# One PSUM copy of each quad moved from VectorE to ScalarE in a window-attention backward kernel

## The chip, the cores and the metric

The kernel runs on one core of a Trainium2 chip. The metric is the time of one execution on the device in microseconds (us); the median of several runs is compared. The engines are named as the profile names them: PE (matrix engine, PEld its weight loads), DVE (VectorE), ACT (ScalarE), POOL (GpSimd) and SP (the sync engine, which here only issues transfers).

## The reference, cut to what matters

```python
def _fwd_reference(x, wqkv, wo):               # x: 1 x 256 x 256 x 384, bf16
    # 1024 windows of 8 x 8 = 64 tokens, C = 384 channels, one head
    qkv = xw @ wqkv
    q, k, v = qkv[..., :C], qkv[..., C:2*C], qkv[..., 2*C:]
    p = softmax(einsum('bqc,bkc->bqk', q, k) * C ** -0.5)
    o = einsum('bqk,bkc->bqc', p, v) @ wo
...
_out, _vjp = jax.vjp(_f, x, wqkv, wo)
return _out, *_vjp(grad_out)                   # o, dx, dwqkv, dwo
```

## The kernel before, in words

**Algebra.** The weights are multiplied together once: A = Wq Wk^T scaled, B = Wv Wo, and their transposes. Then the scores are x A x^T, the output is P (x B), and the gradient of P is grad_out B^T x^T. Both weight gradients come from two sums over all windows, x^T (dS x) and x^T (P^T grad_out), with dS the gradient of the scores; a few small products after the loop turn them into dwqkv and dwo.

**Tiling.** Two windows make a tile of 128 tokens, four tiles (numbered t = 0 to 3) a quad; there are 128 quads. The order of all five engines' instructions is written out by hand: each engine runs its instructions in the order in which the program gives them. One call of `step` works on three quads at once: stage A on quad i+1, stage B on quad i, stage C on quad i-1.

- Stage A: z = B^T grad_out (`project`, kind 0, line 147, copied by ACT at L161), y = A x (`project`, kind 1, L145, copied by ACT at L163), and `to_tokens`, a transposing DMA of both into `tok`.
- Stage B: scores and dP in one tile `sd` (L147), softmax and its gradient on DVE with one exponential on ACT, giving `Pb` (P) and `ps` (P and dS side by side); u = x B and v = x A^T (`uv`, L147, copied by ACT at L229); `turn`, a transposing DMA of `ps` into `PS`.
- Stage C, `attend`, once for the tiles (0, 1) and once for (2, 3), "first pair" and "second pair". For each of the two tiles: dS x in `pu` (to `Uq`), P u in `po` (the output), P^T grad_out in `pw` (to `Wq`), and dx in `pd`. Each of these is four matmuls on 64 x 64 quarters of the array.
- Filler: a sixth of the sum over three finished quads (`pg`, 12 matmuls, or 24 on halves of the array), added into `GF_acc` by DVE (L304), twice per step.

**Order of a step on PE.** `sd`; eight `uv` products; three z products; a `pg` filler; first pair; three y products; a `pg` filler; second pair. So right behind the first pair's last two matmuls (`token_part` of t1, L258) stands the first y product (L145, with `A_sb`).

**Order inside a pair.** PE: `token_part` of t0 (two matmuls into `pd`), `pu` and `po` of t0, `pw` and `pd` of t0, `pu` and `po` of t1, `pw` and `pd` of t1, `token_part` of t1. DVE: the four copies `Uq` t0 (L274), `Wq` t0 (L277), `Uq` t1 (L281), `Wq` t1 (L284). ACT: two copies of `po` (L264 `o`) and two of `pd` (L264 `d`), which end only with the pair. Before the first pair, ACT's last work is the three z copies (L161); after it come the three y copies (L163). DVE's last work before the first pair is the `GF_acc` addition of the filler.

**The ring.** All PSUM tiles come from one ring of eight banks (tag "r"), 33 tiles a step. A tile's first matmul waits until the reader of the bank's former tile is done. The banks are handed out in the order in which the program releases them. In the program before, the first y product takes the bank of the first pair's `pu` t0 (released by the DVE copy L274), the second y product that of the first `po` (ACT), the third that of `pw` t0 (DVE, L277), and the filler behind them that of the second `po` (ACT). In the second pair, `pw` of t1 takes the bank of that filler (released by DVE, L304).

**Transfers.** SP issues, in this order in every step: `dT` and `xT` (transposing DMAs of grad_out and x for the quad after next, L128), `PS` (L233), four loads of x (L118), and `tok` (L167). POOL issues the stores of both outputs after each pair (six each) and four loads of grad_out.

Of the kernel before, what the change touches and what calls it, by code (L numbers as in the profile page):

```python
# [22 lines left out]
def kernel(  # L23
# [21 lines left out]
    nc = tc.nc  # L45
# [61 lines left out]
    def windows(ap, st, first, count=2):  # L107
        row, col = st["at"]
        return ap[0, row + WIN * first:row + WIN * (first + count), col:col + WIN, :]
# [126 lines left out]
    def turned(st, n, t, h):  # L236
        if n in ("PT", "ST"):
            return st["PS"][h, t, int((n == "ST") == (h == LO)), :]
        return st[n][h, t, :]

    def attend(st, pair):
        if pair[0] == 0:
            st["Uq"] = grp.tile([P, QUAD, C], BF16, tag="Uq", name="Uq")
            st["Wq"] = grp.tile([P, QUAD, C], BF16, tag="Wq", name="Wq")

        def bank(name):
            return ring.tile([P, C], F32, tag="r", name=name)

        def both(straight, crossed, t, outer, **flags):
            for h, o, (dst, lhs, rhs), fl in ((LO, LO, straight, {}), (LO, HI, crossed, flags), (HI, LO, crossed, flags),  # L250
                                              (HI, HI, straight, {})):
                at = dst if dst is not crossed[0] else dst[outer if h == LO else 1 - outer]
                nc.tensor.matmul(at[o, :], lhsT=turned(st, lhs, t, h), rhs=st[rhs][h, t, :],  # L253
                                 **{"start": True, "stop": True, **fl})

        def token_part(t, pd, outer, **flags):
            for w, o in ((0, HI), (1, LO)):
                nc.tensor.matmul(pd[outer if w == 0 else 1 - outer][o, :], lhsT=st["ps"][:, t, w, :],  # L258
                                 rhs=st["tok"][:, :, t, w, :], **flags)

        def keep(name, dst, src):
            for outer in (0, 1):
                sb = ob.tile([P, C], BF16, tag=name, name=name)
                nc.scalar.copy(out=sb[:], in_=src[outer][:])  # L264
                stores.append((dst, sb, outer))

        t0, t1 = pair
        stores = []
        pu = [bank("pu")]
        po = [bank("po") for outer in (0, 1)]  # L270
        pd = [bank("pd") for outer in (0, 1)]
        token_part(t0, pd, 1, start=True, stop=False)
        both((pu[0], "ST", "xq"), (po, "PT", "uq"), t0, 1)
        nc.vector.tensor_copy(out=st["Uq"][:, t0, :], in_=pu[0][:])  # L274
        pw = [bank("pw")]
        both((pw[0], "Pb", "dq"), (pd, "ST", "vq"), t0, 1, start=False, stop=True)
        nc.vector.tensor_copy(out=st["Wq"][:, t0, :], in_=pw[0][:])  # L277
        pu.append(bank("pu"))
        both((pu[1], "ST", "xq"), (po, "PT", "uq"), t1, 0)
        keep("o", out_0, po)  # L280
        nc.vector.tensor_copy(out=st["Uq"][:, t1, :], in_=pu[1][:])  # L281
        pw.append(bank("pw"))
        both((pw[1], "Pb", "dq"), (pd, "ST", "vq"), t1, 0, start=True, stop=False)
        nc.vector.tensor_copy(out=st["Wq"][:, t1, :], in_=pw[1][:])  # L284
        token_part(t1, pd, 0, start=False, stop=True)
        keep("d", out_1, pd)
        for dst, sb, outer in stores:
            if outer:
                nc.gpsimd.dma_start(out=windows(dst, st, 2 * t1 + 1, 1), in_=sb[LO, :])
                nc.gpsimd.dma_start(out=windows(dst, st, 2 * t0, 1), in_=sb[HI, :])  # L290
            else:
                nc.gpsimd.dma_start(out=windows(dst, st, 2 * t0 + 1), in_=sb[:])  # L292
# [22 lines left out]
    def step(c, b, a, ahead):  # L315
# [25 lines left out]
        if ahead is not None:  # L341
            load(ahead)
        filler(1)
        C_(attend, (0, 1))
        split[0] = True
        for mo in range(CK):
            A(project, 1, mo)
        A(to_tokens)
        filler(1)
        split[0] = ALL  # L350
        C_(attend, (2, 3))

    G_ON_PE = 0
# [86 lines left out]
```

## Time and profile before

| what | value |
|---|---|
| median of 4 runs | 2007.19 us (2000.94 to 2009.74) |
| the profiled execution | 2007.31 us, of which the span of the trace is 2005.2 us |
| granted TensorE clock | 0.999 |
| PE, PEld busy | 1970.7 us (98%), 1193.8 us (60%) |
| DVE, ACT, POOL busy | 1318.0 us (66%), 1405.4 us (70%), 1122.4 us (56%) |
| DMA packets' time, SP's queue and POOL's queue | 81.3% and 30.9% of 16 engines' span |
| `Uq` copy L274 on DVE | 256 times, mean 553 ns (median 558 in the first pair, 548 in the second) |
| ACT copies of the same shape (128 x 384, f32 to bf16) | `uq` 483 ns, `vq` 488, `o` 482, `d` 505 |

The profile is one execution. Busy shares are averages over the span; a PE that is busy 98% is not at its peak, because the ends of pipelined matmuls are modelled and overlap. What one step costs is read best from the timeline: from one `sd` to the next, 15.2 us pass in most steps. In timeline rows, the columns are start (us), duration (us), engine, line, operation, tiles and shape, count, and in brackets the idle time before and what ended it.

### The profile page before, as it was taken

What the parts mean: (1) busy time and instruction counts of PE and PEld (TensorE: products, weight loads), DVE (VectorE), ACT (ScalarE), POOL (GpSimd) and SP (SyncE); (2) the same over time, 40 slices, a digit from 0 to 9 for tenths busy, and PEclk for the clock granted to TensorE, in tenths of its full rate; (3) what the DMA queues carried; (4) which work ended last, traced back from release to release, by engine and by line L of the source; (5) the groups of instructions that cost most, each with busy time, mean ns of one, the idle gap of its engine ahead of it and who ended that gap; (6) DMA issues with size and microseconds to landing.
All of it is one profiled execution on the core that took longest, in us unless ns stands there. A gap on an engine that the chain in (4) does not pass through costs nothing. (4 is left out here: it accounts for less than half of the span.)

```text
span 2005.2 us, 52374 instructions
## 1 busy us (share of the span) xinstructions
PE 1970.7 (98%) x19418; PEld 1193.8 (60%) x19418; DVE 1318.0 (66%) x2979; ACT 1405.4 (70%) x3213; POOL 1122.4 (56%) x2054
## 2 busy tenths in 40 slices
PE   8899999999999999999999999999999999999998
PEld 4456556665666665656655666666666566666565
DVE  5666666666666666666666666666666666666666
ACT  5777777676767767767777677677767777777773
POOL 3555555555556555555655565555555556555543
PEclk9999999999999999999999999999999999999999
DMA  9999999999999999999999999999999999999993
GB/s 200 221 211 220 196 221 222 220 215 211 211 218 219 216 214 212 226 210 217 220 211 214 218 217 213 220 218 221 217 204 226 207 222 220 219 215 207 222 204 98
DMA packets 1042272, 425.62 MB, mean 212 GB/s; under 512 B 925792, under 2 KB 1016672, under 8 KB 1042016
## 3 DMA queue, kind: packets, MB, share of 16 engines
q1 hardware_dynamic: 943312, 270.60, 81.3%
q0 software_dynamic: 98304, 151.39, 30.9%
q8 instruction: 152, 2.49, 0.5%
q14 instruction: 104, 0.85, 0.1%
q10 hardware_dynamic: 400, 0.29, 0.0%
HBM read 101.84 MB, written 101.84 MB: 102 GB/s over the span
## 5 line engine op out<-in xcount | busy, mean ns | idle before, releaser
L292 POOL DMA_DIRECT2D out_dram<-o x256 | 139.2, 544 | 714.8 <-ACT o L264 703.1
L264 ACT CAST o<-po 128x384 bf16<-128x384 f32 x512 | 220.4, 482 | 375.6 <-PE pu L253 365.1
L304 DVE TENSOR_TENSOR GF_acc<-pg,GF_acc 128x384 f32<-128x384 f32 x258 | 143.9, 558 | 501.7 <-PE pg L145 343.7
L147 PEld LDWEIGHTS <-xT 128*128 128x128 bf16 x3072 | 291.8, 98 | 182.2
L147 PE MATMUL pj<-B_sb,xT 128*128 128x384 bf16 x1536 | 333.4, 326 | 0.0
L147 PE MATMUL pj<-AT_sb,xT 128*128 128x384 bf16 x1536 | 333.3, 326 | 0.0
L119 POOL DMA_DIRECT2D dq<-in_grad_out_dram x512 | 274.2, 547 | 73.1 <-DMA out_dram<-o 40.9
L147 PE MATMUL pj<-dT,BT_sb 128*128 128x512 bf16 x1152 | 269.7, 379 | 12.8 <-DMA dT<-dq 11.2
L145 PE MATMUL pj<-xT,A_sb 128*64 128x512 bf16 x2304 | 274.4, 381 | 0.6 <-DMA xT<-xq 0.6
L229 ACT CAST uq<-pj 128x384 bf16<-128x384 f32 x512 | 247.4, 483 | 30.5 <-PE pj L147 26.9
L229 ACT CAST vq<-pj 128x384 bf16<-128x384 f32 x512 | 250.1, 488 | 2.7 <-ACT uq L229 0.3
L145 PEld LDWEIGHTS <-xq 128*64 128x64 bf16 x3000 | 210.7, 110 | 46.2
L264 ACT CAST d<-pd 128x384 bf16<-128x384 f32 x512 | 225.7, 505 | 0.3 <-ACT o L264 0.2
L147 PEld LDWEIGHTS <-xq 128*128 128x128 bf16 x1572 | 153.7, 98 | 114.8 <-issue 0.3
L163 ACT CAST yz<-pj 128x512 bf16<-128x512 f32 x384 | 206.7, 633 | 2.4 <-PE pj L145 2.3
L161 ACT CAST yz<-pj 128x512 bf16<-128x512 f32 x384 | 207.0, 643 | 1.9 <-ACT vq L229 1.3
L207 ACT COPY ps<-Pb 64x256 bf16<-64x256 bf16 x256 | 103.2, 403 | 149.7 <-DVE Pb L204 148.2
L145 PEld LDWEIGHTS <-A_sb 128*64 128x64 bf16 x2304 | 156.2, 110 | 84.7 <-issue 1.2
L147 PEld LDWEIGHTS <-BT_sb 128*128 128x128 bf16 x1152 | 111.6, 98 | 138.1 <-DMA dT<-dq 17.6
L147 PE MATMUL pg<-Uq,xq 128*128 128x384 bf16 x1032 | 181.6, 326 | 0.0
L258 PE MATMUL pd<-tok,ps 128*64 128x384 bf16 x1024 | 181.4, 344 | 0.0
L253 PE MATMUL pu<-xq,PS 64*64 64x384 bf16 x1024 | 175.0, 335 | 6.2 <-DMA PS<-ps 6.1
(67 smaller groups left out, 3384.9 us busy)
## 6 DMA issues: line engine op xcount, KB each, us to landing
xq<-in_x_dram SPq DMA_DIRECT2D x512, 96.0 KB, 4.1
dq<-in_grad_out_dram POOLq DMA_DIRECT2D x512, 96.0 KB, 3.9
out_dram<-o POOLq DMA_DIRECT2D x256, 96.0 KB, 4.3
out_dram<-o POOLq DMA_DIRECT2D x512, 48.0 KB, 4.3
out_dram<-d POOLq DMA_DIRECT2D x256, 96.0 KB, 4.5
out_dram<-d POOLq DMA_DIRECT2D x512, 48.0 KB, 4.4
dT<-dq SPq DMA_TRANSPOSE x128, 6.5
xT<-xq SPq DMA_TRANSPOSE x128, 6.8
```

Of the source, the lines that this page charges most:

```text
L119: nc.gpsimd.dma_start(out=dq[:, t, :], in_=windows(grad_out, st, 2 * t))
L145: nc.tensor.matmul(out[h], lhsT=lhsT[:, h], rhs=rhs, start=start, stop=stop)
L147: nc.tensor.matmul(out, lhsT=lhsT, rhs=rhs, start=start, stop=stop)
L161: ENG[EV["z"][mo]](out=yz[:, mo, :, 0:4:3, :], in_=pj[:])
L163: ENG[EV["y"][mo]](out=yz[:, mo, :, 1:3, :], in_=pj[:])
L207: nc.scalar.copy(out=ps[h, :, w, :], in_=Pb[h, :, :])
L229: cp(out=dst[:, t, :], in_=pj[:])
L253: nc.tensor.matmul(at[o, :], lhsT=turned(st, lhs, t, h), rhs=st[rhs][h, t, :], **{"start": True, "stop": True, **fl})
L258: nc.tensor.matmul(pd[outer if w == 0 else 1 - outer][o, :], lhsT=st["ps"][:, t, w, :], rhs=st["tok"][:, :, t, w, :], **flags)
L264: nc.scalar.copy(out=sb[:], in_=src[outer][:])
L292: nc.gpsimd.dma_start(out=windows(dst, st, 2 * t0 + 1), in_=sb[:])
L304: nc.vector.tensor_tensor(out=GF_acc[:, f, ma, :], in0=pw[:], in1=GF_acc[:, f, ma, :], op=ALU.add)
```

## The change

The copy of `pu` into `Uq` for the first tile of a pair (L274) goes to ACT where that tile is t0 = 0, that is in the first pair, and stays on DVE in the second pair. 128 of the 256 copies of that line move. In ACT's order the moved copy stands between the third z copy (L161) and the first `o` copy (L264).

```diff
         both((pu[0], "ST", "xq"), (po, "PT", "uq"), t0, 1)
-        nc.vector.tensor_copy(out=st["Uq"][:, t0, :], in_=pu[0][:])
+        (nc.vector.tensor_copy if t0 else nc.scalar.copy)(out=st["Uq"][:, t0, :], in_=pu[0][:])
         pw = [bank("pw")]
```

The order of PE, SP and POOL does not change, nor the number of waits on PE. Because banks are handed out in the order of release, three of them go to other tiles: the first y product still takes the bank of `pu` t0 (now released by ACT), the second takes that of `pw` t0 (DVE, L277), the third that of the first `po` (ACT), the filler that of the second `po` (ACT). In the second pair `pu` t0 takes the bank of the first pair's `pw` t1 (DVE) and one `po` that of a `pd` of the first pair (ACT); before, it was the other way round.

## Prediction, made before the changed kernel ran

> **What bounds the kernel now.** I read the page first, then the chain of waits, the list of PE's waits, the timeline around the change, and last SP's timeline, because the DMA figure looked suspicious.
>
> ```profile
> span 2005.2 us, 52374 instructions
> PE 1970.7 (98%) x19418; PEld 1193.8 (60%) x19418; DVE 1318.0 (66%) x2979; ACT 1405.4 (70%) x3213; POOL 1122.4 (56%) x2054
> ```
>
> ```profile
> PE pj L147 <- DMA dT<-dq: 11.2, 8, 2.6
> ...
> PE pu L253 <- DMA PS<-ps: 6.1, 5, 2.0
> ```
>
> PE is busy 98%, and the chain that ended last is PE work all through the loop. PE's listed waits (the second fence: us in total, times, longest) are few: 17.3 us for transfers in 13 places of the loop. DVE and ACT have a third of their time free, so what their copies cost in busy time says nothing; what counts is when a copy frees a PSUM bank that PE wants. Such waits need not show in a list of idle time, since modelled ends of matmuls overlap the next start. I therefore looked at starts, around the first pair of one step:
>
> ```profile
> 1006.78 0.56 DVE L304 TENSOR_TENSOR GF_acc<-pg,GF_acc 128x384 f32<-128x384 f32 x1 [1.11 <-PE pg L147]
> ...
> 1006.97 0.35 PE L253 MATMUL pu<-xq,PS 64*64 64x384 bf16 x1
> ...
> 1007.37 0.56 DVE L274 CAST Uq<-pu 128x384 bf16<-128x384 f32 x1
> ...
> 1007.67 0.86 ACT L264 CAST o<-po 128x384 bf16<-128x384 f32 x2 [0.72 <-PE pu L253]
> 1007.73 0.35 PE L258 MATMUL pd<-tok,ps 128*64 128x384 bf16 x2
> ...
> 1007.98 1.27 PE L145 MATMUL pj<-xT,A_sb 128*64 128x512 bf16 x10
> ```
>
> The copy L274 ends at 1007.37 + 0.56 = 1007.93, and 0.05 us later the first y product starts, the tile that takes over this bank. In the trace's records, to the nanosecond, this holds in all 123 undisturbed steps: the product starts 53 to 55 ns after the copy's end, whatever else varies. So it waits for the copy. What would it do if it didn't? Three steps show it, because in them the copy was done early (198 to 1632 ns ahead of the product); this is one:
>
> ```profile
> 69.06 0.56 DVE L274 CAST Uq<-pu 128x384 bf16<-128x384 f32 x1 [0.78 <-PE pu L253]
> ...
> 69.96 0.35 PE L258 MATMUL pd<-tok,ps 128*64 128x384 bf16 x2
> ...
> 70.15 1.68 PE L145 MATMUL pj<-xT,A_sb 128*64 128x512 bf16 x14
> ```
>
> From the second of the two L258 matmuls to the product it is 183, 184 and 184 ns in these three, against 242 to 245 ns (median 243) in the 123 others. The hidden wait is 243 - 183 = 60 ns a step. The steps run at 15,206 ns with a scatter of 1 to 2 ns except where a transfer is late, so such a wait is paid each time.
>
> I computed the same distance, from a bank's release to its next matmul, for all 33 tiles of a step. One other tile is held: `pw` of t1 in the second pair, 54 ns behind the `GF_acc` addition. The next smallest distances are 130 ns (`pw` of t1 in the first pair, behind `GF_acc`) and 161 ns (`sd`, behind the second pair's L274), and then 353 ns.
>
> **What is removed, and what stays.** DVE loses 128 copies of 558 ns, of which its order needs 465 (start to start of the copies behind it). DVE had them between the `GF_acc` addition and `Wq` of t0. It is 66% busy, so this alone is worth nothing. `Wq` of t0 could start 0.3 us earlier; its bank's next user had 881 ns to spare, and as second y product it will still have about 490.
>
> **What is added, and when it is done.** The matmuls of `pu` t0 end, as modelled, 52 ns before DVE starts (1007.32). DVE starts later than it could, because the `GF_acc` addition ends only at 1007.34; on other occasions DVE starts 37 ns behind PE. ACT's shortest distance behind PE is 36 ns. ACT has been idle by then for 413 ns (median, from the end of the third z copy to the start of L274), so it starts about 15 ns earlier than DVE. It then takes 478 to 485 ns for this shape (the `o` and first `uq` copies, whose mean in the page is 482 and 483) against 558. So the bank is free 15 + 75 = 90 ns earlier. From an ACT copy's end to a waiting matmul it is 52 ns (seen at the start of the trace), as from DVE. The product would thus be held for 60 - 90 = -30 ns: no longer at all, and the limit is PE's own 183 ns. Gain: 60 ns, with 30 ns of margin. Bounds: were the ACT copy as slow as the `d` copies (505) or the fourth `uq` (498), the margin shrinks to 10 ns and the gain stays; at 0.55 us it would be 40 ns less. So 20 to 60 ns, and I take 60, the row of the plain copy.
>
> The Trainium skill ("Perfetto Trace Analysis", Optimizing Scalar/DVE Operations) gives an access overhead of about 125 ns for DVE on PSUM and 51 for ACT, twice that in profiled latency. By that, as an estimate, the ACT copy would be 2 x 74 = 148 ns shorter; the rows say 75. The sum would be the same 60 ns, since PE's own 183 ns ends it. The same section would offload to ACT when DVE is saturated; here ACT is the busier one (70% against 66%), so by that advice there is nothing to gain, and what speaks for the change is only the bubble.
>
> **What is pushed back.** On ACT the two `o` copies, two `d` copies and three y copies queue behind the moved one. ACT's copies follow each other at 370 to 375 ns, so the first `o` starts at about 9.65 us after `sd` instead of 9.59: 60 ns later. Who waits for them: the third y product has the first `o`'s bank (it had 471 ns as second product and now comes 650 ns later, so about 1000 ns), the filler the second `o`'s (about 1250). The y copies start about 60 ns later until the third, which waits for PE (its product ends within 20 ns of its start now) and so moves with PE. Its readers, `sd` and the DMA `tok`, see nothing. POOL's stores of the first pair start 60 ns later; POOL idles 4.54 us before them. Cost: 0. In the second pair the swapped banks had 2.8 us to spare.
>
> **Sum.** 123 steps x 60 ns = 7.4 us at PE. The profiled execution took 2007.31 us, 0.1 above the median of 2007.19, so either can be the base: 2007.3 - 7.4 = 1999.9 if all of it arrives.
>
> **What may take it back: the transfers.** SP's timeline is solid:
>
> ```profile
> 999.37 1.19 SPq L233 DMA_TRANSPOSE PS<-ps  x1
> 1000.61 2.50 SPq L118 DMA_DIRECT2D xq<-in_x_dram  x4
> 1003.22 5.40 SPq L167 DMA_TRANSPOSE tok<-yz  x1
> 1008.85 1.92 SPq L128 DMA_TRANSPOSE dT<-dq  x1
> 1010.95 3.73 SPq L128 DMA_TRANSPOSE xT<-xq  x1
> 1014.84 1.19 SPq L233 DMA_TRANSPOSE PS<-ps  x1
> ```
>
> One round follows the other with gaps of 0.04 to 0.23 us, and SP waits for nobody; `PS` is issued 7 to 8 us before PE needs it, with 4.7 us to land. About every thirteenth round takes 18.5 us instead of 15, and most of PE's waits for `dT` or `PS` follow one of these. So SP and PE are nearly balanced. Is SP the true limit? The Trainium skill ("Perfetto Trace Analysis", What "DMA-bound" means) counts a solid issuing track as one of the ways to be bound by DMA; by that the gain would be 0. The trace speaks against it: issue durations stretch and shrink. The five kinds' shortest issues (4.04, 1.41, 1.42, 1.19, 4 x 0.58 us) and gaps sum to 11.2 us. When `PS` is 6.5 to 7.0 us ahead, a round takes 14.7 us in the mean; at 7.5 to 8.0 us, 15.25; above 8, 15.6. SP thus catches up when it falls behind, and 15.15 us a round is inside what it does. Its lead would settle some 0.2 us lower (0.06 us over a slope of 0.33 us a round for each us of lead). Each of 13 waits may grow by up to that, 2.6 us, but most waits have their own jitter; I take 0.5. Bounds: 0, and all 7.4.
>
> Forecast: 2007.3 - 7.4 + 0.5 = 2000.4 us.
>
> **Rivals.**
> - *The transfers keep the time.* SP's mean round, long ones included, is 15.32 us, as is PE's with its waits. If that is a capacity, PE's 60 ns turn into longer waits: 2004 to 2008 us, PE's listed DMA waits rising from 17 towards 25 us. For it: SP never idles. Against: the fast rounds after each long one.
> - *The wait isn't one, or ACT only replaces it.* Either 243 ns is PE's own change between tilings, or ACT frees the bank no earlier. Time 2007. Against the first: three steps at 183; against the second: 75 ns in duration. It would need an ACT copy of over 0.56 us.
> - *Slower: ACT arrives late at the copy.* The place is ACT's queue ahead of L274, the three z copies. They end 0.41 us before `pu` is ready. If they or a wait for the third z copy's `yz` push L274 by more than 0.09 + 0.41 = 0.50 us, the y product waits longer than now, and each further 0.1 us costs 12.3 us: 2013 us at 0.05 beyond. It decides against me only if the z copies move, and nothing in the diff moves them.
>
> **How the numbers follow.** About 0.3% (6 us, 2001.2) is what a measurement of this kernel can tell from no change; single runs before lie 4.4 us around their middle. Bank wait gone and mostly kept: 0.75, giving 1997 to 2003, with 0.63 below 2001.2 and 0.12 above. Transfers keep it: 0.13 (0.11 same, 0.02 slower). No real wait: 0.06, same. ACT late: 0.06, slower. Together faster 0.63, same 0.29, slower 0.08. The likeliest case's own range is 1997 to 2003; to hold 8 in 10 with the transfers' case and run scatter I take 1996.5 to 2007.
>
> **What would show it.** After: L274 on ACT 478 to 505 ns, starting 0.3 to 0.5 us behind the third z copy; 183 to 190 ns from L258 to the first y product; `pw` of t1 in the second pair still 54 ns behind `GF_acc`; steps of 15.146 us; first `o` about 0.06 us later within the step; PE's DMA waits 17 to 21 us. Wrong, if the y product still starts 50 to 55 ns behind the copy, now ACT's, or if the steps are 15.15 us but late transfers eat over 4 us.

## The result, and the profile after

The changed kernel takes 1998.73 us (median of 44 runs) against 2005.66 us for the kernel before, now over 70 runs. The ratio is 0.9968, with a 95% interval of 0.9957 to 0.9979: 6.4 us less. The forecast was 6.9 us less, from a base of 2007.3 us to 2000.4; of the 1.7 us between 2000.4 and 1998.73, 1.5 are the base, which came out at 2005.66 over more runs. The profiled execution has a span of 1998.1 us against 2005.2. The row of busy times of the page after:

```profile
PE 1963.3 (98%) x19418; PEld 1122.8 (56%) x19418; DVE 1258.4 (63%) x2851; ACT 1453.9 (73%) x3341; POOL 1122.4 (56%) x2054
```

DVE lost 60 us of busy time, ACT took on 49, and PE is busy 98% as before. None of these shares tells of a gain. PEld's fall by 71 us is a trace of it, as the third experiment shows. The timeline after, around the first pair of one step, answers to the one of before:

```profile
1015.28 0.35 PE L253 MATMUL pu<-xq,PS 64*64 64x384 bf16 x1
...
1015.68 0.48 ACT L274 CAST Uq<-pu 128x384 bf16<-128x384 f32 x1 [0.41 <-PE pu L253]
...
1016.05 0.35 PE L258 MATMUL pd<-tok,ps 128*64 128x384 bf16 x2
1016.06 0.87 ACT L264 CAST o<-po 128x384 bf16<-128x384 f32 x2
...
1016.24 2.11 PE L145 MATMUL pj<-xT,A_sb 128*64 128x512 bf16 x18
```

The copy ends at 1016.16 and the y product starts 0.08 us later. In the records it is 73 to 75 ns in all undisturbed steps, where a matmul that waits for a copy follows at 51 to 55. From L258 to the product it is now 183 or 184 ns in all of them, against 243: the wait is gone. The usual step went from 15,206 to 15,129 ns, which is 77 ns and not 60.

PE's listed waits hardly moved in their sum, 17.1 us against 17.3, but stand in 19 places instead of 13 (before: 11.2 us for `dT` in 8 places, 6.1 for `PS` in 5):

```profile
PE pu L253 <- DMA PS<-ps: 10.8, 10, 2.7
...
PE pj L147 <- DMA dT<-dq: 6.3, 9, 1.4
```

### The profile page after: what moved, and what is told of

Same layout as the page of the kernel before. It is cut to its first block, busy times and chain, and to the rows that moved or that the text cites. A ratio compares the mean times of both kernels' runs of the same rounds, so it can differ in the third digit from the quotient of the medians.

```text
span 1998.1 us, 52374 instructions
## 1 busy us (share of the span) xinstructions
PE 1963.3 (98%) x19418; PEld 1122.8 (56%) x19418; DVE 1258.4 (63%) x2851; ACT 1453.9 (73%) x3341; POOL 1122.4 (56%) x2054
## 5 line engine op out<-in xcount | busy, mean ns | idle before, releaser
L264 ACT CAST o<-po 128x384 bf16<-128x384 f32 x512 | 221.3, 487 | 248.3 <-issue 247.7
L264 ACT CAST d<-pd 128x384 bf16<-128x384 f32 x512 | 227.5, 512 | 0.2 <-ACT o L264 0.2
L145 PEld LDWEIGHTS <-xq 128*64 128x64 bf16 x3000 | 167.8, 110 | 88.9
L161 ACT CAST yz<-pj 128x512 bf16<-128x512 f32 x384 | 206.6, 644 | 0.5 <-ACT vq L229 0.2
L145 PEld LDWEIGHTS <-A_sb 128*64 128x64 bf16 x2304 | 132.6, 110 | 98.9 <-issue 1.9
L258 PE MATMUL pd<-tok,ps 128*64 128x384 bf16 x1024 | 177.7, 344 | 0.0
```

The lines of the kernel that those rows point to most:

```text
L145: nc.tensor.matmul(out[h], lhsT=lhsT[:, h], rhs=rhs, start=start, stop=stop)
L161: ENG[EV["z"][mo]](out=yz[:, mo, :, 0:4:3, :], in_=pj[:])
```

## The experiments

Ratios are to the kernel before, run on the same chip. "Late" is what the steps of the profiled execution, from the sixth on, take above their usual length, summed; most of it is waiting for `dT` or `PS`. It comes from one execution of each kernel. (In e5 and e6 the usual step itself holds such waits.)

| kernel | ratio (95%) | usual step, ns | late, us |
|---|---|---|---|
| before | 1 | 15,206 | 14.4 |
| the change | 0.9968 (0.9957 to 0.9979) | 15,129 | 16.3 |
| e1, second pair only | 0.9999 (0.9980 to 1.0019) | 15,204 | 12.6 |
| e2, both pairs | 0.9971 (0.9954 to 0.9988) | 15,129 | 19.3 |
| e3, 64 columns late | 1.0005 (0.9985 to 1.0024) | 15,238 | 12.7 |
| e4, 384 columns late | 1.0154 (1.0126 to 1.0183) | 15,504 | 10.0 |
| e5, before, x loads on POOL | 1.1362 (1.1326 to 1.1399) | 17,085 | 54.7 |
| e6, change, x loads on POOL | 1.1340 (1.1311 to 1.1368) | 16,592 | 105.5 |
| e7, second filler whole | 1.0028 (1.0009 to 1.0046) | 15,280 | 8.3 |
| e8, before, no `d` stores | 0.9920 (0.9898 to 0.9942) | 15,206 | -0.1 |
| e9, change, no `d` stores | 0.9873 (0.9852 to 0.9894) | 15,129 | 0.0 |
| e10, second filler by ACT | 0.9936 (0.9914 to 0.9958) | 15,102 | 14.8 |

**Is it this bank, or the engines' load?**

```diff
-        nc.vector.tensor_copy(out=st["Uq"][:, t0, :], in_=pu[0][:])
+        (nc.scalar.copy if t0 else nc.vector.tensor_copy)(out=st["Uq"][:, t0, :], in_=pu[0][:])   # e1
+        nc.scalar.copy(out=st["Uq"][:, t0, :], in_=pu[0][:])                                      # e2
```

> The copy goes to ACT in the second pair only; the first pair's stays on DVE. Theory (only the bank that the first y product takes over matters): the first y product still starts 53 to 55 ns behind DVE's copy and 243 ns behind the L258 matmul, steps of 15.206 us, ratio to before 0.998 to 1.002; the second pair's copy frees a bank for sd that had 161 ns to spare. Rival (a copy less on DVE, or ACT's shorter copy, is worth something wherever it stands): about the same gain as the change, ratio 0.995 to 0.998.

> All 256 copies on ACT. Theory: the same as the change, steps of 15.129 us, ratio 0.995 to 0.999. Rival (load of DVE and ACT): twice the gain of the change, ratio 0.992 to 0.995, or a loss because ACT is busy by three quarters.

Both went as the theory has it. In e1 the first pair's timeline is that of before:

```profile
1005.11 0.56 DVE L274 CAST Uq<-pu 128x384 bf16<-128x384 f32 x1
...
1005.47 0.35 PE L258 MATMUL pd<-tok,ps 128*64 128x384 bf16 x2
...
1005.72 2.13 PE L145 MATMUL pj<-xT,A_sb 128*64 128x512 bf16 x18
```

The product stands 0.05 us behind the copy (54 ns in the records). The second pair's copy, also 80 ns earlier, only gave `sd` 242 ns to spare instead of 161. So 128 copies fewer on DVE are worth nothing by themselves that the runs can tell, and 256 on ACT bring no more than 128.

**Does the release time set the product's start?** In e3 and e4, ACT first copies 64 or 384 columns of the same PSUM tile to a scratch tile.

```diff
+        if t0 == 0:
+            scr = ob.tile([P, C], BF16, tag="scr", name="scr", bufs=2)
+            nc.scalar.copy(out=scr[:, 0:64], in_=pu[0][:, 0:64])     # e4: 0:384
         (nc.vector.tensor_copy if t0 else nc.scalar.copy)(out=st["Uq"][:, t0, :], in_=pu[0][:])
```

> As the change, but ACT first copies 64 columns of the same PSUM tile to scratch, so that the real copy starts later. From copies of 512 columns at 477 ns start to start and of 384 at 370, 64 columns take 103 ns. Theory: release and y product 103 - 19 = 84 ns later than after the change, the product 53 ns behind the copy again, its two halves 29 ns apart again, steps of about 15.23 us (15.129 + 0.084 + 0.017 for the halves), ratio to before 1.000 to 1.003. Rival (the gain comes from relieving DVE): the gain stays, ratio 0.995 to 0.998.

> As the change, but ACT first copies the whole PSUM tile to scratch, 370 ns more. Theory: the y product 351 ns later than after the change, steps of 15.497 us, 123 x 0.29 = 36 us over before less what the transfers' waits (about 15 us) give back: 2027 to 2042 us, ratio 1.011 to 1.018. Rival (the distance of 243 ns is the matrix engine's own and no wait): the ACT queue takes 370 ns in its idle time, ratio 0.996 to 1.000.

The timeline of e3 (L276 is the scratch copy, L277 the moved one):

```profile
1021.83 0.21 ACT L276 CAST scr<-pu 128x64 bf16<-128x64 f32 x1 [0.41 <-PE pu L253]
...
1021.94 0.48 ACT L277 CAST Uq<-pu 128x384 bf16<-128x384 f32 x1
...
1022.20 0.35 PE L258 MATMUL pd<-tok,ps 128*64 128x384 bf16 x2
...
1022.47 2.13 PE L145 MATMUL pj<-xT,A_sb 128*64 128x512 bf16 x18
```

In e3 the product comes 51 ns behind the copy again, 276 ns behind L258, 93 ns later than after the change (84 expected), and the gain is gone although DVE has 128 copies fewer. In e4 it comes 543 ns behind L258, 359 ns later than after the change (351 expected). The expectations had put the delay of the copy at 103 and 370 ns; in the records it starts 109 and 376 ns later than after the change and, being 7 ns longer, ends 117 and 383 ns later. Between the two, 266 ns more delay made the product 266 ns later: a slope of one, behind a flat part of 24 ns. In e3 PE's matmuls wait for the same engines in the same order as after the change, so the three banks that go to other tiles are not what brings the gain. e4's list of PE's waits (us in total, times, longest) is instructive:

```profile
PE pj L145 <- ACT Uq L277: 23.7, 123, 0.2
```

It names 0.2 us a step, where the starts show 0.36 above the free 183 ns; the shorter waits of before, of 60 ns a step, are not in that list at all.

e3 and e4 also show where the further 17 ns come from. The y products run as two matmuls on the array's halves. When the first of them had to wait, the two halves' matmuls run about 29 ns apart from the second pair of them on, through the filler, to the two L258 matmuls of the second pair (30 ns apart), and `pu` follows 256 ns behind the later one. When it did not wait, they are 2 ns apart there. Summed over the way from the y product to `pu` of the second pair this is 23 ns (4176 against 4153); 6 ns go back at the next held tile. In e3, which waits again, the offset (30 ns), the 4175 ns and PEld's 1193 us are back. That a wait brings the offset is shown; why the halves then keep 29 ns was not.

**Where does part of the gain stay?** 123 steps of 77 ns are 9.5 us; the runs show 6.4 (4.2 to 8.6). I suspected the transfers and first took the four loads of x from SP's solid round.

```diff
-            nc.sync.dma_start(out=xq[:, t, :], in_=windows(x, st, 2 * t))
+            nc.gpsimd.dma_start(out=xq[:, t, :], in_=windows(x, st, 2 * t))
```

> The kernel before, with the four loads of x per step issued by POOL in place of SP, so that SP's round loses 2.3 to 2.8 us of issues. It asks where the rest of the gain stays. Theory A (SP's solid track is why PE sometimes waits for dT and PS): these waits of 15 us go to under 5, steps stay 15.206 us, time 1991 to 1997, ratio 0.993 to 0.997. Theory B (the 16 DMA engines are full and set the transfers' pace): waits as before, ratio 0.998 to 1.003.

> The changed kernel with the loads of x on POOL. Theory A: PE's full 77 ns a step arrive, 123 x 0.077 = 9.5 us below the same kernel without the change: 1982 to 1988, ratio to before 0.988 to 0.992. Theory B: as the change alone, ratio 0.995 to 0.999.

Neither theory foresaw this: over 13% slower. In e5, PE waits 204 us for `PS` and `dT`, and the chain of waits goes through these transfers (us in total, times, longest):

```profile
PE pu L253 <- DMA PS<-ps: 106.2, 64, 4.6
PE pj L147 <- DMA dT<-dq: 98.0, 59, 4.8
```

SP's track, here in its timeline, is no longer solid:

```profile
1001.87 5.62 SPq L167 DMA_TRANSPOSE tok<-yz  x1
1011.46 2.17 SPq L128 DMA_TRANSPOSE dT<-dq  x1
```

SP waits 4 us before `dT`, which is the median of 95 such holes. In at least half of them it waits for a load of grad_out: in the records of 47, `dT` starts less than 0.14 us behind the landing of one. These loads queue on POOL behind stores and now also among the loads of x. POOL, which in the kernel before waited for ACT, now waits for landings (78 us for `xq` loads in one row of its waits). Not all of the 270 us more are waits: the granted clock is 0.971 in this execution, against 0.999 before, and PE's busy time is 70 us longer. The run says that these loads don't belong there, not what limits SP. Nor does the pair e5 and e6 say whether PE's 77 ns arrive where the transfers set the pace: the ratios, 1.1362 and 1.1340, have overlapping intervals, and the 0.0047 of a full gain fits in them as well as none.

So I relieved the transfers by leaving stores out, on both kernels.

```diff
         for dst, sb, outer in stores:
+            if dst is out_1 and st["i"]:
+                continue
```

> The kernel before without the stores of the d tiles (the gradient of x stays unstored but for the first quad): 50 MB of 426 MB and 6 of 16 POOL issues per step left out. It relieves the transfers and touches nothing on PE, ACT or DVE. Theory (late transfers take back part of what PE gains): steps of 15.206 us stay, PE's time over these steps goes from 14 us to under 6, ratio to before 0.993 to 0.997. Rival (the transfers' waits have nothing to do with their load): ratio 0.998 to 1.001.

> The changed kernel without the stores of the d tiles, to be compared with the kernel before without them. Theory: with the transfers relieved, the full 123 x 0.077 = 9.5 us arrive, 0.47% between the two, ratio to before 0.988 to 0.992. Rival (the missing third of the gain was lost elsewhere): again 6 to 7 us between the two, ratio 0.990 to 0.994 at most.

With 50 MB less to move the late steps vanish (-0.1 and 0.0 us), and the medians are 1991.22 and 1981.27 us: 9.95 us apart, and the ratios 0.0047 (each known to 0.0022), where 9.5 us were expected. The runs of the two kernels do not overlap (1989.16 to 1993.72, 1980.49 to 1983.71). So the full 77 ns arrive when the transfers have room, and with all stores about a third does not (9.5 - 6.4 = 3.1 us; by the interval of the 6.4 it is 0.9 to 5.3). SP's timeline in e8 is in places as solid as before:

```profile
1016.07 1.19 SPq L233 DMA_TRANSPOSE PS<-ps  x1
1017.31 2.63 SPq L118 DMA_DIRECT2D xq<-in_x_dram  x4
1020.04 5.02 SPq L167 DMA_TRANSPOSE tok<-yz  x1
1025.29 1.55 SPq L128 DMA_TRANSPOSE dT<-dq  x1
1027.01 3.27 SPq L128 DMA_TRANSPOSE xT<-xq  x1
```

In other places it has holes (rows of SP, and of the two copies that it waits for):

```profile
1225.66 2.51 SPq L118 DMA_DIRECT2D xq<-in_x_dram  x4
...
1227.71 1.61 ACT L163 CAST yz<-pj 128x512 bf16<-128x512 f32 x3
...
1229.35 3.60 SPq L167 DMA_TRANSPOSE tok<-yz  x1
...
1235.65 2.87 SPq L128 DMA_TRANSPOSE xT<-xq  x1
...
1238.58 0.85 DVE L219 TENSOR_TENSOR ps<-pr,pd 64x256 bf16<-64x256 f32 x2
...
1239.58 1.19 SPq L233 DMA_TRANSPOSE PS<-ps  x1
```

Ahead of `tok` SP is idle for 1.2 us and ahead of `PS` for 1.1, and each starts 0.03 and 0.15 us behind the end of what it moves: SP has caught up and waits for ACT and DVE. In the records from 200 to 1900 us, e8 has 80 such places in 112 rounds and e9 has 88. The kernel before has none: there each `PS` is issued at least 7.3 us behind the `ps` that it moves. So SP's track was solid before because SP ran behind its producers. Its own issues are the same in e8, and yet those of a round take 13.7 us in the mean instead of 14.4. Only stores of POOL went, so the length of SP's issues depends on the other queue's transfers; through what they share was not tried.

The Trainium skill ("Perfetto Trace Analysis", What "DMA-bound" means) counts a solid issuing track as one of the ways to be bound by DMA. Here the sign holds in part: the track is solid in all kernels of the table that have late steps (e5 and e6 aside), and has holes in the two that have none; but two thirds of the gain arrived with the track solid.

The other rows fit: a longer step leaves the transfers more room. e4's step adds 123 x 0.298 = 36.7 us and its ratio only 31; e7's adds 9.1 and its ratio 5.6; late time falls to 10.0 and 8.3 us.

**The other held tile.** A tile is held when its first matmul waits for the bank's former reader. `pw` of t1 in the second pair still starts 54 ns behind the `GF_acc` addition (204 ns behind its forerunner, where 153 are free).

```diff
-        filler(1)
         split[0] = ALL
+        filler(1)                        # e7
         C_(attend, (2, 3))
```

> The changed kernel with the second filler of a step in 12 whole-array matmuls in place of 24 on halves of the array. It goes at the other held tile, pw of t1 in the second pair, 54 ns behind the GF_acc addition. Its last matmul would then end some 100 ns earlier against the pair, as in the first filler, so that hold of about 51 ns should go. But PE then changes its tiling twice more: behind the y products, and ahead of the pair, where L258 follows at 256 ns instead of 161. Theory: no gain, 0 to 100 ns a step more, ratio to before 0.997 to 1.004. Rival (only the hold counts): 51 ns a step less than the change, ratio 0.993 to 0.995.

The hold went (153 ns, 129 to spare), but the filler starts 311 ns behind the y products instead of 214, and L258 follows at 255 instead of 161: the step is 151 ns longer than after the change, half as much again as the loss that was feared.

```diff
-                nc.vector.tensor_tensor(out=GF_acc[:, f, ma, :], in0=pw[:], in1=GF_acc[:, f, ma, :], op=ALU.add)
+                src = pw
+                if split[0]:             # the second filler of a step
+                    src = sm.tile([P, C], F32, tag="sg", name="sg")
+                    nc.scalar.copy(out=src[:], in_=pw[:])
+                late.append((f, ma, src))
+                if not split[0]:
+                    add_late()           # makes the additions in `late`; called also ahead of the next first filler
...
```

> The changed kernel, and the second filler's PSUM tile is copied to SBUF by ACT, which frees its bank; DVE adds it to GF_acc from there in the next step, ahead of the first filler. It goes at the other held tile without changing PE's tiling. ACT's 478 ns against DVE's 557 free the bank 79 ns earlier, the hold is 51 ns (204 against 153). Theory: pw of t1 at 153 ns with some 80 ns to spare, steps of about 15.08 us, 6 us less at PE, two thirds of it in the time: ratio to before 0.993 to 0.996. Rival (ACT's 128 further copies or DVE's later addition hold something else): ratio 0.996 or above.

This version beats both kernels: 1995.32 us, ratio 0.9936, though its interval just touches that of the change. The step is 15,102 ns; 27 of the 51 ns of hold are gone (177 ns behind the forerunner instead of 204), not all, because ACT's copy starts late (timeline of e10):

```profile
1006.25 0.48 ACT L313 COPY sg<-pg 128x384 f32<-128x384 f32 x1 [1.23 <-PE pg L145]
```

Its 478 ns are as expected, but it starts 99 ns (median) behind the filler's last matmul, where DVE's addition started 37 (before) and 44 (after the change) behind it. It waits for two semaphores, PE's and ACT's own, where the moved L274 waits for one and starts at 51. That the second wait costs the 50 ns is likely and was not tried by itself.

## Why the prediction was right, point by point

- *The hidden wait of 60 ns behind L274:* right. The three early steps gave the free distance (183 ns) exactly, and the whole loop now has it. (How early the copy was in them I had read wrongly: the records give 528, 528 and 671 ns, which changes nothing.)
- *When ACT is done:* the size was a little off. ACT starts 51 ns behind `pu`, as DVE did (52), not 36, so the 15 ns of an earlier start were not there: DVE's `GF_acc` addition had not held the copy. The copy took 478 ns. The margin is 20 to 24 ns instead of 30; the gain does not depend on it.
- *What is pushed back on ACT, and the swapped banks, at 0:* right. The third y product has 991 ns to spare and the filler 1255, against 1000 and 1250.
- *The sum of 7.4 us at PE:* undersized. The step fell by 77 ns, 9.5 us in all; the halves' offset, 17 ns net, was in the trace of before (gaps of 186 and 29 ns in the held products, 213 and 3 in the free ones) and I had not carried it through to the second pair.
- *The transfers, 0.5 us:* undersized as well. They took about 3 us (9.5 - 6.4). I had argued that SP's lead would settle 0.2 us lower and that most of the 13 waits would not feel it; their number rose from 13 to 19, at smaller size. The profiled executions, one of each kernel, show 1.9 us of the 3 as late time (16.3 against 14.4). The bound of 2.6 us that I gave was nearer than the value I took. The reading behind it was too kind to SP: it never idled because it ran at least 7.3 us behind DVE, and e8 and e9 show it catching up once stores are left out. Its long rounds I had also miscounted: 7 of 127 are over 17 us, not one in thirteen of 18.5.
- The two errors, 2 to 3 us each, cancel, and that is luck. The forecast of a gain of 6.9 us came out at its size with both terms short; that there is a gain rests on the first alone.
- *The rivals:* that there is no real wait is excluded by e3 and e4; that ACT comes late is excluded by the margin of about 20 ns that every undisturbed step shows. That the transfers keep all of it is excluded by the ratio; that they keep what is missing is shown by e8 and e9, its size of a third only roughly.

## What to carry to other kernels

When PE is busy 98%, compare the distance between two matmuls in the usual step with the same distance in the odd step where the suspected producer was early, and look for a producer that ends at a constant distance ahead of a start. A list of idle time does not show a wait of 60 ns. Then ask who else is nearly late: a gain at PE is only as large as what the transfers let through, and leaving out some stores on both kernels shows that share directly. For an issuing queue whose track is solid, compare the start of an issue with the end of what it moves: 7.3 us and more behind, as here before, means that the queue is late, and not only that it is occupied.

## What the runs showed of the hardware that was not expected

- A product that runs on two halves of the array keeps a wait of its first matmul as an offset of 29 ns between the halves for the 42 matmuls of the y products and the filler; PEld's busy time (1193.8 us with it, 1122.8 without) shows it on the page.
- Four loads per step moved from SP to POOL cost over 13%, although POOL was busy only 56%: POOL then waits for landings, SP for POOL's loads (holes of 4 us, at least half of them), PE for SP's transfers (204 us), and the granted clock is 0.971 instead of 0.999.
- With 12% of the bytes left out, all of them stores of POOL's queue, SP's unchanged issues took 13.7 us a round instead of 14.4, SP caught up with ACT and DVE, and all late steps vanished: the length of an issue depends on the other queue's transfers.
